# Batch 0 of a spectral-mixing kernel: filter halves copied by GpSimd and DMA, two-bank blocks, and rings in place of pools

## The chip, the cores and the metric

The kernel runs on one core of one Trainium2 chip. The metric is the device time of one execution in microseconds (us). The kernel before takes 776.99 us, the median of three runs (776.98 to 777.12).

The engines are called here as the profile calls them: PE is the TensorE matmul, PEld its weight load, DVE the VectorE, ACT the ScalarE, POOL the GpSimd, SP the SyncE, whose queue only issues transfers. A line number such as L501 is a line of the kernel before; PSUM is the memory that matmuls write, in eight banks of 512 float32 per partition.

## The reference

For eight batches of 3008 tokens with 256 channels, a real Fourier transform along the tokens, a product with a complex filter, and the inverse transform; then, for all 24064 tokens, a layer of width 2048 with a snake activation and a projection back to 256.

```
X = np.fft.rfft(x, axis=1)
F = (filt_r + 1j * filt_i)[None, :, :]
y = np.fft.irfft(X * F, n=x.shape[1], axis=1)
...
h = x @ w_in
s = np.sin(alpha * h)
g = h + s * s / (alpha + 1e-09)
out = g @ w_out
```

## The kernel before, in words

The transform of length 3008 is split as 47 x 64. A first small transform runs over 47 points (`wf_t`), giving 24 classes `s` of real and imaginary parts; a second one runs over 64 points per class (`d_t`), and its result lies with real parts on partitions 0 to 63 and imaginary parts on 64 to 127. There the filter is applied, and the two inverse transforms follow (`e_t`, then `wi_t`). What comes out is `y`, channels on partitions.

**The main loop.** `chunks` are pieces of 512 (or 384) tokens of `y`. For a chunk `k`, `hidden(k, jb)` makes 128 of the 2048 hidden columns: two matmuls into one bank (L601), a cosine on ACT (L605), a combination on DVE (L606). `project(k - 1, u)` multiplies the chunk before with `w2` (L621), ACT copies the result (L630), and POOL's queue stores it. One step of the loop is two `hidden` and the matching `project`. The transforms of batches 1 to 7 are planned into these steps by hand: `put(at, fn)` gives each piece a step number, `slot` issues what is due. Each engine works off its own instructions in the order in which they are issued.

**The head.** Batch 0 has no batch before it to hide beside, so its transform is the head of the program. In order: 16 first matmuls with evictions (L459, L185/L187); four transposes on DVE (`turn`, L473); for 12 blocks of four classes and one half of the channels (`hc`), `forward_0` (four matmuls into one bank of the `hps` pool, L491, then an ACT eviction into `xf0`, L495), `product_0` (one DVE instruction of 1024 elements per partition that multiplies `xf0` with both filter tiles, L501) and `inverse_0` (eight matmuls into a bank of the `fps` pool, L513, then an ACT eviction, L185); two large transposes back (`turn_back`, L473); then the last transform (`last_0`, L403) and the first `hidden`. Blocks 0 to 5 use classes 0 to 11, blocks 6 to 11 classes 12 to 23. `warm_pe(n)` issues n matmuls on zeros that nothing reads (L437). `inverse_table` (L426, L428) makes `e1_0`, the inverse table for the crossed products, by transposing `d_t` and scaling it with -0.125 on ACT.

**The filter.** A real-by-complex product needs the real filter on both partition halves and the imaginary one on both halves, with opposite signs. The load brings each into one half only (`filt_t`, L364: classes 0 to 11 as g = 0, classes 12 to 23 as g = 1). `other_half(g, k)` makes the other half on DVE, by a copy for the real part (L187) and a multiplication with -1 for the imaginary part (L445). The two for g = 0 stand between and behind the four transposes, the two for g = 1 around product 5.

**The weights.** SP's queue loads six parts of `w_in` (L526), the first after the real filter of g = 1 has landed, then four tables and `w_out` (L536). POOL scales `w_in` into `w1` (`weights_in`, L542), held back until the last product of batch 0, and `w_out` into `w2` (`weights_out`, L574).

**Batches 1 to 7** use `forward` (ACT evicts into `xf`, L246, then two transfers on SP's queue swap the partition halves into `xs`, L250), `product` (L257), `cross` (L263, L264) and an inverse. `xf` comes from a pool of three buffers, `xs` of three, `p` of seven. Batch 1 has its twelve `forward` 1.21 steps apart, batch 2 has them 2.2 steps apart, later ones 4.

Of the kernel before, what the change touches and what calls it, by code (L numbers as in the profile page):

```python
# [71 lines left out]
def kernel(  # L72
# [38 lines left out]
    xfpool = pool("xf", 3)  # L111
    ppool = pool("pp", 7)
    xspool = pool("xs", 3)
# [4 lines left out]
    fps = pool("fps", 2, PSUM)  # L118
    hps = pool("hps", 4, PSUM)
    ops = pool("ops", 2, PSUM)  # L120
# [31 lines left out]
    f_t = [filt_t[:, k] for k in range(2)]  # L152

# [35 lines left out]
    class Spectral:  # L189
# [13 lines left out]
        def first(self, i):  # L203
            ch, j = divmod(i, 4)
            ps = fps.tile([128, 512], FP32, name=f"pa_{self.b}_{i}", tag="f")
            marks["pe"] = nc.tensor.matmul(out=ps[0:NK, :], lhsT=wf_t, rhs=self.x[ch][:, 2 * j:2 * j + 2, :],  # L206
                                           start=True, stop=True)
            r0 = 8 * (ch % 2)
            evac(t1_h[ch // 2][0:NK, r0 + 2 * j:r0 + 2 * j + 2, :], ps[0:NK, :])
            if j == 3:  # L210
                nc.sync.dma_start(out=self.d1_rows[:, 8 * ch:8 * ch + 8, :], 
                                  in_=t1_h[ch // 2][0:NK, r0:r0 + 8, :])

        def first_tiled(self, ch):
            r0 = 8 * (ch % 2)
            for q in range(2):
                own, tag = (hps, "h") if q else (fps, "f")
                ps = [own.tile([128, 512], FP32, name=f"pa_{self.b}_{ch}_{q}_{h}", tag=tag) for h in range(2)]
# [19 lines left out]
        def forward(self, u):  # L238
            b = self.b
            ps = fps.tile([128, 2, C], FP32, name=f"pb_{b}_{u}", tag="f")  # L240
# [4 lines left out]
            self.xf[u] = xfpool.tile([128, 2, C], FP16, name=f"xf_{b}_{u}", tag="xf")  # L245
            nc.scalar.copy(out=self.xf[u], in_=ps)  # L246
            if self.fused:
                self.xs[u] = xspool.tile([128, 2, C], FP16, name=f"xs_{b}_{u}", tag="xs")
                for p in range(2):
                    nc.sync.dma_start(out=self.xs[u][64 * p:64 * p + 64, :, :],  # L250
                                      in_=self.xf[u][64 - 64 * p:128 - 64 * p, :, :])

        def product(self, u):
            self.p[u] = []
            for k in range(1 if self.fused else 2):
                pt = ppool.tile([128, 2, C], FP16, name=f"p_{self.b}_{u}_{k}", tag="p")
# [9 lines left out]
        def inverse(self, w):  # L266
# [4 lines left out]
            ps = fps.tile([128, 2, C], FP32, name=f"pc_{b}_{w}", tag="f")  # L271
# [12 lines left out]
        def inverse_tiled(self, w):  # L284
            g = gpool.tile([128, 4, 2, C], FP16, name=f"gt_{self.b}_{w}", tag="g")
            for q in range(2):
                own, tag = (hps, "h") if q else (fps, "f")
                ps = [own.tile([128, 2, C], FP32, name=f"pc_{self.b}_{w}_{q}_{k}", tag=tag) for k in range(2)]
# [20 lines left out]
        def last(self, u):  # L309
# [3 lines left out]
            ps = fps.tile([128, 4, 128], FP32, name=f"pd_{self.b}_{u}", tag="f")  # L313
            psv = ps.rearrange("p a b -> p (a b)")[:, 0:4 * NR].rearrange("p (a r) -> p a r", r=NR)
# [20 lines left out]
    one = cpool.tile([128, 16], BF16)  # L335
    for t in [one] + parts:
        nc.gpsimd.memset(t, 0.0)
# [10 lines left out]
    def spread_alpha(i):  # L348

        ps = hps.tile([128, 4, 128], FP32, name=f"al_bc_{i}", tag="h")  # L350
# [42 lines left out]
    def last_0(n0, n, own=fps, tag="f", spread=False):  # L393

        for cb in range(2):
            made = []

            def one(i, cb=cb, made=made):

                if i == 0:  # L400
                    ps = own.tile([128, 512], FP32, name=f"pd_0_{n0}_{cb}", tag=tag)
                    made.append(ps[:, 0:n * NR].rearrange("p (a r) -> p a r", r=NR))
# [11 lines left out]
    def reciprocals():  # L414

        ps = ops.tile([128, 512], FP32, name="ps_rec", tag="o")
# [3 lines left out]
    def inverse_table(g):  # L420

        gs = slice(8 * g, 8 * g + 8)
        ps = ops.tile([128, 8, 128], FP16, name=f"pse_{g}", tag="o")
# [4 lines left out]
        nc.scalar.mul(e1_0[:, gs, :], ps, -0.125)  # L428

    warmed = []  # L430

    def warm_pe(n):

        warmed.append(n)
        ps = hps.tile([128, 512], FP32, name=f"warm_{len(warmed)}", tag="h")
# [3 lines left out]
    def other_half(g, k, on_act):  # L439

        gs = slice(12 * g, 12 * g + 12)
        if k == 0:
            evac(f_t[0][64:128, gs, :], f_t[0][0:64, gs, :], on_act)
        else:
            nc.vector.tensor_scalar(out=f_t[1][0:64, gs, :], in0=f_t[1][64:128, gs, :],  # L445
                                    scalar1=-1.0, scalar2=None, op0=ALU.mult)
# [9 lines left out]
    for i in range(16):  # L456
        own, tag = (fps, "f") if i % 3 == 2 else (hps, "h")
        ps = own.tile([128, 512], FP32, name=f"pa_0_{i}", tag=tag)
# [21 lines left out]
    for i in range(4):  # L480
        turn(t2_0[i // 2][:, :, 32 * (i % 2):32 * (i % 2) + 32], t1_0[:, :, 32 * i:32 * i + 32])
        if i > 1:
            other_half(0, i - 2, False)
    blocks = [(hc, w) for hc in range(2) for w in range(3)] + [(0, 3), (1, 3), (0, 4), (0, 5), (1, 4), (1, 5)]
    xf0, p0 = {}, {}

    def forward_0(i):
        hc, w = blocks[i]
        ps = hps.tile([128, 4, 128], FP32, name=f"pb_0_{i}", tag="h")
        for j in range(4):  # L490
            nc.tensor.matmul(out=ps[:, j, :], lhsT=d_t[:, 4 * w + j, :],  # L491
                             rhs=t2_0[hc][:, 4 * w + j], start=True, stop=True)
        own, tag = (xspool, "xs") if i % 2 else (xfpool, "xf")
        xf0[i] = own.tile([128, 4, 128], FP16, name=f"xf_0_{i}", tag=tag)
# [3 lines left out]
    def product_0(i):  # L498
        hc, w = blocks[i]
        p0[i] = xpool.tile([128, 2, 4, 128], FP16, name=f"p_0_{i}", tag="x")  # L500
        marks["products"] = nc.vector.tensor_tensor(  # L501
            out=p0[i].rearrange("p f s (k c) -> p f s k c", k=2),
            in0=xf0[i].rearrange("p s (k c) -> p s k c", k=2)[:, None].to_broadcast([128, 2, 4, 2, 64]),
            in1=filt_t[:, :, 4 * w:4 * w + 4].rearrange("p f s (k c) -> p f s k c", k=2)[..., 64 * hc:64 * hc + 64],
            op=ALU.mult)

    def inverse_0(i):
        hc, w = blocks[i]
        ps = fps.tile([128, 4, 128], FP32, name=f"pc_0_{i}", tag="f")
        for j in range(4):  # L510
            s = 4 * w + j
            for k in range(2):
                nc.tensor.matmul(out=ps[:, j, :], rhs=p0[i][:, k, j, :],  # L513
                                 lhsT=e_t[:, s, :] if k == 0 else e1_0[:, s, :],
                                 start=(k == 0), stop=(k == 1))
        evac(g_0[hc][:, 4 * w:4 * w + 4], ps.rearrange("p s (k c) -> p s c k", k=2), not (i in ()))

    after(nc.sync.dma_start(out=wi0_t, in_=wi0_dram.ap()), marks["filt", 0, 1])
    w_in_v = moe_w_in.rearrange("(a p) j -> p a j", p=128)
    w_in32 = []  # L520
    for g in range(6):
# [5 lines left out]
        if g == 0:  # L527
            after(ins, marks["filt", 1, 0])
        marks["w_in"] = ins
# [18 lines left out]
    [inverse_table(g) for g in range(2)]  # L548
    for i in range(6):
        forward_0(i)  # L550
        if i % 3 == 2:
            if i == 2: inverse_table(2)
            warm_pe((4, 0)[i // 3])
    for i in range(13):
        for e in {5: [(1,0,False)],6: [(1,1,False)]}.get(i, ()):
            other_half(*e)
        if i < 12:
            product_0(i)
        if i == 11:
# [3 lines left out]
        if i + 6 < 12:  # L563
            forward_0(i + 6)
        if i == 12:
            turn_back(0)
# [16 lines left out]
    warm_pe(12)  # L583
    last_0(0, 4)
    last_0(4, 2, hps, "h")
# [8 lines left out]
    def hidden(k, jb):  # L594
# [4 lines left out]
        ps = hps.tile([128, 512], FP32, name=f"ph_{k}_{jb}", tag="h")  # L599
# [10 lines left out]
    def project(k, u):  # L610
# [7 lines left out]
        if (t % 2 == 0 or alone) and half == 0:  # L618
            pso[k] = ops.tile([128, 2, C], FP32, name=f"po_{k}_{t}", tag="o")
# [73 lines left out]
    for at, fn in put_later:  # L693
        put(at, fn)

# [3 lines left out]
    for n0, n, at in ((6, 5, 1.5), (11, 4, 11), (15, 4, 13), (19, 4, 15.5), (23, 4, 17), (27, 5, 19)):  # L699
        put(at, last_0, n0, n, fps, "f", True)  # L700
# [91 lines left out]
```

## Time and profile before

| what | value |
|---|---|
| median of three runs | 776.99 us |
| the profiled execution's own time | 779.76 us |
| its span in the trace | 778.0 us |
| PE / DVE / ACT / POOL busy | 98% / 85% / 78% / 48% |
| start of the first `last_0` matmul (L403) | 36.98 us |
| start of the first `hidden` matmul (L601) | 38.53 us |

Busy shares are of the whole span. The head is its first 39 us, where the limits are others than in the rest, so it is read by itself: from the rows in order of time, which give the start, the length, the engine, the line, what is written and read, the count, and in brackets the engine's idle time before and what ended it. The profile is of one execution on the one core.

### The profile page before, as it was taken

How to read it: one execution, taken by the hardware profiler on the slowest of the kernel's cores; microseconds unless marked ns; L12 is line 12 of the kernel's file. 1: busy time of each engine (PE TensorE's matmuls, PEld its weight loads, DVE VectorE, ACT ScalarE, POOL GpSimd, SP SyncE). 2: the span in 40 equal slices, each digit the busy share in tenths (PEclk: the TensorE clock that was granted, in tenths of full speed). 3: DMA queues.
4: the chain of work that ended last, by engine and by line, in shares of the span. 5: the costliest groups of instructions: out<-in, count | busy, mean ns of one | idle time of the engine just before them, and what ended most of it. 6: DMA issues, size and time to landing. Idle time of an engine off the chain costs nothing.

```text
span 778.0 us, 17230 instructions
## 1 busy us (share of the span) xinstructions
PE 764.5 (98%) x6039; PEld 517.0 (66%) x6039; DVE 658.0 (85%) x1174; ACT 610.4 (78%) x1204; POOL 370.4 (48%) x649
## 2 busy tenths in 40 slices
PE   7999999999999999999999999999999999999997
PEld 3757766666666666666666666766666666766665
DVE  6986998999988888898889988898888888787773
ACT  5798888898878877888878787788778787777762
POOL 6355555634555655455464647554454645430000
PEclk9999999999999999999999999999999999999999
DMA  9955578864765428644474536864254322511112
GB/s 223 267 108 160 119 181 242 220 137 124 187 165 133 124 58 219 154 108 127 107 194 121 139 95 145 198 152 120 72 145 110 87 70 56 135 46 34 37 41 56
DMA packets 81518, 101.49 MB, mean 130 GB/s; under 512 B 18884, under 2 KB 60864, under 8 KB 81431
## 3 DMA queue, kind: packets, MB, share of 16 engines
q0 software_dynamic: 27440, 47.29, 26.1%
q1 hardware_dynamic: 53434, 52.79, 25.4%
q8 instruction: 47, 0.77, 0.4%
q10 hardware_dynamic: 557, 0.31, 0.2%
q14 instruction: 40, 0.33, 0.1%
HBM read 56.15 MB, written 46.66 MB: 132 GB/s over the span
## 4 chain that ended last, share of the span: by engine, by line
PE 91%; DVE 5%; ACT 1%; issue 1%; DMA 1%; ACTq 0%; DVEq 0%
PE po L621 40%; PE ph L601 40%; DVE v L606 3%; PE pd L316 2%; PE pb L243 2%; PE pa L222 2%; PE pc L293 1%; ACT cos_all L605 1%; PE pc L513 1%; DMA w<-in_moe_alpha_dram 1%; PE warm L437 1%; PE pb L491 1%; PE pa L459 1%; PE pa L206 0%; PE pd L403 0%
## 5 line engine op out<-in xcount | busy, mean ns | idle before, releaser
L606 DVE SCALAR_TENSOR_TENSOR v<-cos_all,ph 128x512 f16<-128x512 f32 (+1 forms) x768 | 482.5, 671 | 99.2 <-ACT cos_all L605 95.7
L605 ACT ACTIVATE cos_all<-ph 128x512 f32<-128x512 f32 (+1 forms) x768 | 413.9, 600 | 101.8 <-PE ph L601 98.5
L665 POOL DMA_DIRECT2D out_dram<-o x530 | 291.7, 557 | 244.1 <-ACT o L630 215.3
L621 PE MATMUL po<-w,v 128*128 128x256 f16 x3008 | 389.9, 273 | 0.9 <-DVE v L606 0.9
L601 PE MATMUL ph<-y,w 128*128 128x512 f16 (+1 forms) x1536 | 389.1, 375 | 1.3 <-DVE v L606 1.1
L621 PEld LDWEIGHTS <-v 128*128 128x128 f16 x3008 | 289.9, 98 | 85.9 <-DVE v L606 1.5
L601 PEld LDWEIGHTS <-w 128*128 128x128 f16 x1536 | 143.1, 98 | 114.0 <-issue 19.1
L630 ACT COPY o<-po 128x512 f32<-128x512 f32 (+1 forms) x95 | 56.1, 591 | 7.6 <-PE po L621 6.9
L246 ACT CAST xf<-pb 128x512 f16<-128x512 f32 x84 | 51.1, 608 | 2.0 <-PE pb L243 1.2
L185 ACT CAST y<-pd 128x376 f16<-128x376 f32 (+1 forms) x86 | 42.1, 491 | 12.3 <-PE pd L316 8.8
L160 POOL DMA_DIRECT2D x<-in_x_dram x48 | 25.6, 538 | 40.1 <-DVE v L606 26.8
L185 ACT CAST t_h<-pa 128x512 f16<-128x512 f32 (+1 forms) x60 | 32.8, 590 | 12.5 <-PE pa L222 11.3
L316 PEld LDWEIGHTS <-t_a 96*128 96x128 f16 x448 | 31.4, 97 | 12.7
L264 DVE TENSOR_TENSOR p<-p,xs 128x512 f16<-128x512 f16 x84 | 35.7, 425 | 2.9
L263 DVE TENSOR_TENSOR xs<-xs,filt_t 128x512 f16<-128x512 f16 x84 | 35.1, 418 | 1.6 <-DMA xs<-xf 1.6
L257 DVE TENSOR_TENSOR p<-xf,filt_t 128x512 f16<-128x512 f16 x84 | 35.0, 417 | 0.0
L185 ACT CAST gt<-pc 128x512 f16<-128x512 f32 x54 | 28.1, 595 | 8.4 <-PE pc L293 8.4
L187 DVE CAST t_h<-pa 128x512 f16<-128x512 f32 (+1 forms) x52 | 33.5, 682 | 0.2
L243 PE MATMUL pb<-t,d_t 128*128 128x256 f16 x168 | 32.1, 273 | 0.6 <-ACT cos_all L605 0.6
L316 PE MATMUL pd<-wh_t,t_a 96*128 96x94 f16 x384 | 31.8, 204 | 0.0
L235 POOL DMA_DIRECT2D t<-d x28 | 24.4, 874 | 12.0 <-DMA d<-t_h 10.9
L243 PEld LDWEIGHTS <-d_t 128*128 128x128 f16 x168 | 16.3, 98 | 15.1 <-DMA t<-d 0.8
(70 smaller groups left out, 278.0 us busy)
## 6 DMA issues: line engine op xcount, KB each, us to landing
t<-d POOLq DMA_DIRECT2D x28, 384.0 KB, 5.2
xs<-xf SPq DMA_DIRECT2D x168, 64.0 KB
t_a<-d SPq DMA_DIRECT2D x28, 384.0 KB
x<-in_x_dram POOLq DMA_DIRECT2D x50, 188.0 KB, 4.5
d<-t_h SPq DMA_DIRECT2D x48, 192.0 KB
d<-gt SPq DMA_DIRECT2D x36, 256.0 KB
out_dram<-o POOLq DMA_DIRECT2D x91, 64.0 KB, 2.1
out_dram<-o POOLq DMA_DIRECT2D x31, 80.0 KB, 3.6
```

Of the source, the lines that this page charges most:

```text
L185: marks["act"] = nc.scalar.copy(out=dst, in_=src)
L243: nc.tensor.matmul(out=ps[:, i, :], lhsT=d_t[:, s, :], rhs=self.t2[s // 6][:, s % 6, :], start=True, stop=True)
L246: nc.scalar.copy(out=self.xf[u], in_=ps)
L263: nc.vector.tensor_tensor(out=xs, in0=xs, in1=f_t[1][:, 2 * u:2 * u + 2, :], op=ALU.mult)
L264: nc.vector.tensor_tensor(out=p, in0=p, in1=xs, op=ALU.add)
L316: nc.tensor.matmul(out=psv[:, i, :], rhs=wi_t if self.b < TILED else wh_t, start=True, stop=True, lhsT=t4_h[ch // 2][0:NK, n0 % 16 + i, cb ...
L601: nc.tensor.matmul(out=ps[:, 0:n], lhsT=w1[:, cb, jb * 128:jb * 128 + 128], rhs=y_cols[:, cb, c0:c0 + n], start=(cb == 0), stop=(cb == 1))
L605: nc.scalar.activation(out=cs[:, 0:n], in_=ps[:, 0:n], func=AFT.Sin, bias=float(np.pi / 2))
L606: marks["snake"] = nc.vector.scalar_tensor_tensor(out=v[k][:, jb, 0:n], in0=cs[:, 0:n], scalar=-1.0, in1=ps[:, 0:n], op0=ALU.add, op1=ALU. ...
L621: nc.tensor.matmul(out=pso[k][:, t % 2, :], lhsT=v[k][:, jb, 128 * t:128 * t + 128], rhs=w2[:, jb, :], start=(jb == 0), stop=(jb == 15))
L630: copy(out=o[:, i0:t % 2 + 1, :], in_=pso[k][:, i0:t % 2 + 1, :])
L665: queues[i % len(queues)].dma_start(out=bass.AP(tensor=out.tensor, offset=out.offset + t0 * C, ap=[*ap, [1, C]]), in_=o_blk[p0:p0 + rows, :])
```

## The change

- **Filter halves.** `other_half(g, k)` now copies without a sign, as 1536 uint32 elements of 64 partitions. For g = 0 POOL does both copies, issued behind the four transposes. For g = 1 both are transfers on SP's queue: the real one behind the load of `wi0_t` and ahead of `w_in`, the imaginary one between the first and the second part of `w_in`.
- **The sign.** `inverse_table` multiplies with a column `sign` (0.125 on partitions 0 to 63, -0.125 on the others; two memsets on DVE at the start), so that batch 0 needs no negated filter. Batches 1 to 7 do: `negate(g)` does it later, on POOL, in place, at steps 8 and 9 of the main loop.
- **Blocks.** Batch 0 goes in eight blocks of 8 and 4 classes in turn. A block of 8 fills two neighbouring banks; one ACT instruction evicts both. `product_0` is two DVE instructions, one per filter tile. `inverse_0` goes into the two `fps` banks (blocks of 8) or one of the two `ops` banks (blocks of 4). The inverse of block 4 is evicted by DVE, the others by ACT. `forward_0` runs four blocks ahead instead of six.
- **Rings.** One PSUM tile of eight banks, with `Ring.take` handing out banks in turn, replaces the three pools of 2, 4 and 2 banks. One tile `work` of 13 pieces replaces the pools `xf` (3), `xs` (3) and `pp` (7): `xf` now has 2 pieces, `xs` 4, `p` 7; batch 0 uses the same pieces.
- **Warm-up.** `warm_pe(12)` ahead of `last_0` becomes `warm_pe(8)`.

```
+    psum = pool("psum", 1, PSUM).tile([128, 8, 512], FP32, name="psum")
+        def take(self, n=1):
+            at = -(-self.at // n) * n % self.n
+            self.at = (at + n) % self.n
+            return psum[:, self.first + at:self.first + at + n].rearrange("p b c -> p (b c)")
+    fps, hps, ops = Ring(0, 2), Ring(2, 4), Ring(6, 2)
...
+    work = cpool.tile([128, 13, 512], FP16)
+    pieces = work.rearrange("p n (i c) -> p n i c", c=C)
...
-            self.xf[u] = xfpool.tile([128, 2, C], FP16, name=f"xf_{b}_{u}", tag="xf")
+            self.xf[u] = pieces[:, u % 2]
...
-                self.xs[u] = xspool.tile([128, 2, C], FP16, name=f"xs_{b}_{u}", tag="xs")
+                self.xs[u] = pieces[:, 2 + u % 4]
...
-                pt = ppool.tile([128, 2, C], FP16, name=f"p_{self.b}_{u}_{k}", tag="p")
+                pt = pieces[:, 6 + (12 * self.b + u) % 7]
...
-        nc.scalar.mul(e1_0[:, gs, :], ps, -0.125)
+        nc.scalar.mul(e1_0[:, gs, :], ps, sign)
...
-    def other_half(g, k, on_act):
+    def other_half(g, k, copy):
+        src = slice(64 * k, 64 * k + 64)
+        dst = slice(64 - 64 * k, 128 - 64 * k)
         gs = slice(12 * g, 12 * g + 12)
-        if k == 0:
-            evac(f_t[0][64:128, gs, :], f_t[0][0:64, gs, :], on_act)
-        else:
-            nc.vector.tensor_scalar(out=f_t[1][0:64, gs, :], in0=f_t[1][64:128, gs, :],
-                                    scalar1=-1.0, scalar2=None, op0=ALU.mult)
+        return copy(out=filt_t[dst, k, gs].rearrange("p s c -> p (s c)").bitcast(UINT32),
+                    in_=filt_t[src, k, gs].rearrange("p s c -> p (s c)").bitcast(UINT32))
+    def negate(g):
+        gs = slice(12 * g, 12 * g + 12)
+        nc.gpsimd.tensor_scalar(out=f_t[1][0:64, gs, :], in0=f_t[1][0:64, gs, :], scalar1=-1.0, scalar2=None,
+                                op0=ALU.mult)
...
-        if i > 1:
-            other_half(0, i - 2, False)
-    blocks = [(hc, w) for hc in range(2) for w in range(3)] + [(0, 3), (1, 3), (0, 4), (0, 5), (1, 4), (1, 5)]
+    for k in range(2):
+        other_half(0, k, nc.gpsimd.tensor_copy)
+    blocks = [(hc, s0, n) for g in range(2) for hc in range(2) for s0, n in ((12 * g, 8), (12 * g + 8, 4))]
...
+        ps = hps.take(n // 4).rearrange("p (s c) -> p s c", c=128)
+        xf0[i] = work[:, 2 * (i % 6):2 * (i % 6) + n // 4].rearrange("p b (s c) -> p (b s) c", c=128)
...
+        for f in range(2):
+            marks["products"] = nc.vector.tensor_tensor(
+                out=p0[i][:, f].rearrange("p s (k c) -> p s k c", k=2),
+                in0=xf0[i].rearrange("p s (k c) -> p s k c", k=2),
+                in1=f_t[f][:, s0:s0 + n].rearrange("p s (k c) -> p s k c", k=2)[..., 64 * hc:64 * hc + 64],
+                op=ALU.mult)
...
+        ps = (ops if i % 2 else fps).take(n // 4).rearrange("p (s c) -> p s c", c=128)
...
+        evac(g_0[hc][:, s0:s0 + n], ps.rearrange("p s (k c) -> p s c k", k=2), i != 4)
...
     after(nc.sync.dma_start(out=wi0_t, in_=wi0_dram.ap()), marks["filt", 0, 1])
+    other_half(1, 0, nc.sync.dma_start)
...
         if g == 0:
             after(ins, marks["filt", 1, 0])
+            other_half(1, 1, nc.sync.dma_start)
...
+    inverse_table(0)
+    inverse_table(1)
+    forward_0(0)
+    forward_0(1)
+    inverse_table(2)
+    warm_pe(4)
+    forward_0(2)
+    forward_0(3)
+    for i in range(9):
+        if i < 8:
             product_0(i)
-        if i == 11:
+        if i == 7:
             reciprocals()
         if i > 0:
             inverse_0(i - 1)
-        if i + 6 < 12:
-            forward_0(i + 6)
+        if i + 4 < 8:
+            forward_0(i + 4)
+    turn_back(0)
     turn_back(1)
...
-    warm_pe(12)
+    warm_pe(8)
...
+    for g in range(2):
+        put(8 + g, negate, g)
```

## The prediction, made before the result was known

> **What bounds the kernel now.** I read the page's shares and chain first, then the rows of the head in order of time for DVE, ACT and SP, then windows of PE with the granted clock, then ACT's waits around batch 1.
>
> From the page:
>
> ```profile
> PE 764.5 (98%) x6039; PEld 517.0 (66%) x6039; DVE 658.0 (85%) x1174; ACT 610.4 (78%) x1204; POOL 370.4 (48%) x649
> ...
> PE 91%; DVE 5%; ACT 1%; issue 1%; DMA 1%; ACTq 0%; DVEq 0%
> ```
>
> PE is the bound over the span, so the loop pays only for what makes PE idle. What the change does to the head counts by one point: when the last transform of batch 0 (L403, 36.98 us) can start. DVE's rows in order of time:
>
> ```profile
> 18.02 1.20 DVE L473 STREAM_TRANSPOSE t<-t 128x1024 uint32<-128x1024 uint32 x1
> 19.23 0.95 DVE L187 COPY filt_t<-filt_t 64x3072 f16<-64x3072 f16 x1
> 20.20 1.25 DVE L473 STREAM_TRANSPOSE t<-t 128x1024 uint32<-128x1024 uint32 x1
> 21.48 0.96 DVE L445 TENSOR_SCALAR filt_t<-filt_t 64x3072 f16<-64x3072 f16 x1
> 22.54 3.10 DVE L501 TENSOR_TENSOR p<-xf,filt_t 128x1024 f16<-128x1024 f16 x5
> 25.67 0.95 DVE L187 COPY filt_t<-filt_t 64x3072 f16<-64x3072 f16 x1
> ...
> 32.42 4.50 DVE L473 STREAM_TRANSPOSE t_a<-t_h 128x2048 uint32<-128x2048 uint32 x2 [0.16 <-ACT t_h L185]
> ```
>
> DVE is never idle for long from 15.7 to 36.92, and L403 follows 0.06 later: here DVE is the bound. ACT, however, is full beside it:
>
> ```profile
> 17.05 1.94 ACT L428 ACTIVATE t_a<-pse 128x1024 f16<-128x1024 f16 x2 [0.20 <-PE pse L426]
> 22.15 2.05 ACT L495 CAST xf<-pb 128x512 f16<-128x512 f32 x4 [0.78 <-PE pb L491]
> ```
>
> Two starts of 512 elements lie 0.48 apart, (2.05 - 0.61) / 3; two of 1024 lie 0.86 apart (1.94 - 1.08). A block of 1024 saves 0.10 against two of 512.
>
> SP, and two windows of PE (start:end, busy, matmuls, clock, DMA share, GB/s):
>
> ```profile
> 17.86 0.36 SPq L518 DMA_DIRECT2D wi_t<-wi_tbl  x1
> 20.97 3.68 SPq L526 DMA_DIRECT2D w_in<-in_moe_w_in_dram  x6
> ```
> ```profile
> 5.00:9.00 4.00, 2.17 (x9) 0.96 1.07 212
> 9.00:12.00 3.00, 3.00 (x8) 0.50 1.09 311
> ```
>
> 17.86 and 20.97 are when the imaginary filter of g = 0 and the real one of g = 1 had landed. The second window shows that a stretch with PE about half busy was followed by 3 us at half clock.
>
> **The change, part by part.**
>
> *DVE's copies go.* Four instructions, 0.95 + 0.96 + 0.95 + 0.96 = 3.82 us. Added: two 64-row memsets (0.06 each, by the 128x1 memset of L321; they delay the first warm-up matmul, not its successors, which wait for x); products, 12 of 0.62 become 8 of 0.62 and 8 of 0.35 (0.62 less 512 elements at 0.53 us), +0.35; the eviction of block 4, 1.25 (0.69 for 512 elements plus 0.56, by the slope between the y casts of 188 and 376). DVE's own work falls by 2.1 us. The fourth transpose ends at 20.48 instead of 21.45.
>
> *POOL's two copies, 1536 elements each.* No such row. Lower bound 1.4 us: casts of 16 and 128 elements take 0.19 and 0.28, 0.8 ns an element. Upper 3.4: the two-input rows of L542, 2.1 ns an element (768 against 512). I take 1.4, the one-input row. POOL has issued its last load at 16.73: copies end at 18.2 and 19.6, before DVE wants them at 20.5. At 3.4 the second ends at 23.5 and costs about 1 us.
>
> *ACT.* Twenty-four evictions of 512 become 7 of 1024 and 8 of 512: 11.5 to 9.9 us. The pointer `sign` on three tables: 0 to 0.1 each, taken 0.1. From 17.05 ACT must do three tables (2.9), six evictions of 1024 (5.3) and four of 512 (1.9) until the inverse of block 2 has left the two fps banks: 27.2. Block 4's inverse needs these banks, DVE's eviction waits for it, and products 6 and 7 are queued behind that eviction. So without any late transfer: inverse 4 at 27.3 to 28.2, eviction to 29.5, products 6 and 7 (1.94) to 31.45, 0.25 to the transposes as now, 4.5: 36.2, a gain of 0.7.
>
> *SP's copy of the imaginary half, g = 1.* This replaces a DVE instruction that ran at once when its load had landed. The load's last issue on POOL is at 15.5; its semaphore in the trace ends at 24.35, as the page's 8.5 us to landing gives. The copy of 393 KB can be issued no earlier. Lower bound: the fastest swap of batch 1 (64 KB, SP, SBUF to SBUF) took 1.9 us; 329 KB more at the 295 GB/s of 22 to 26 us, 1.1; landed at 27.4. Upper: the first part of `w_in`, 393 KB on the same queue, took 5.1 (20.97 to 26.09 by its semaphore); landed at 29.5. I take 27.9, nearer the lower, since the competing POOL queue has landed its last at 25.1. Then: product 4's second half to 28.5, inverse 4 28.65 to 29.55, eviction to 30.9, products 6 and 7 to 32.85, transposes 33.1 to 37.6. Against 36.92: **0.7 late** (0.2 to 2.3). The real half is issued at 21 and, by the 5.1 above, is there at about 26: in front of that.
>
> *Behind it on SP:* `w_in` 1 to 5 go out 3 us later (issue 24.8 instead of 21.4) behind 786 KB more; the last, landed at 31.8 before, lands near 35. POOL wants part 1 at 34, part 5 at 42 (L542): hidden, with 3 us to spare at part 1. `w_out` (39.2 before) at about 41.5; wanted at 44.1.
>
> *PE's clock.* PE waits from 26.4 to 28.65 and, after inverse 5, from about 29.4 to 32.3. From 29.2 to 32.6 it is busy some 1.1 of 3.4 us, less than the 2.17 of 4 that were followed by half clock. I take it that 3.4 us from 32.6 run at half speed: the rest of inverse 6 to 33.8, inverse 7 to 34.7, the alpha matmuls (24 of 0.056) to 36.7, eight warm-ups of 0.216 to 38.4. L403 is behind these in PE's order: 38.4 instead of 36.98, so the head is **1.4 late**, the clock's 0.8 over DVE's 0.7. Without the fall, PE is through at 36.7 and DVE's 37.6 decides.
>
> The Trainium skill, "TensorE: Matmul & The Clock Gate", Part 1, has a free-running activity window of 3.4 us after which an idle PE runs at 1.2 GHz; the trace agrees (half clock for 3 of 3 us from 9 on). By that rule 1.4 late; with a warm clock 0.7.
>
> *`xf` with two buffers.* Batch 1:
>
> ```profile
> ACT xf L246 <- DMA xs<-xf: 0.4, 1, 0.4
> ```
>
> With three buffers ACT waits once, for 0.4: eviction 9 (98.24) for the swaps of 6 (landed 98.14). With two it waits for the swaps of 7, landed 100.85, 2.4 later; eviction 8 (95.74) for those of 6, 2.4, less 1.2 because the fourth `xs` lets them go out earlier; eviction 10 (101.32) for those of 8, 0.9. Queued behind it on ACT are the cosines, and PE runs on by the banks it still has: at 1.7 takes of two fps banks a step of 2.2 us, about 2.5. So PE loses 0 to 2.4; I take **0.4**, since most lies under PE's lead. Batches 2 to 7 are 2.2 or 4 steps apart: nothing.
>
> *Negation on POOL*, two of 3072 elements at 0.8 ns, 2.6 each (6.5 at 2.1 ns). POOL is idle from 49.7 to 58.8 and the loads of `t` start at 69.6: hidden either way. If the cover were gone, out stores would wait 4 us, which three `o` buffers take.
>
> The Trainium skill, "SBUF — State Buffer", on the shared port pair, has GpSimd and a DVE operation with two SBUF inputs exclude each other; between 49.7 and 60 DVE's operations (L606, one input in PSUM) are none of these, and L606 keeps its 0.6 us beside L542. By that rule nothing is lost here.
>
> Rings leave PE's waits in the loop as they were: in the built program 702 hidden matmuls wait for DVE instead of 705.
>
> **Sum.** Head +1.4, `xf` +0.4: **+1.8 us**. The profiled execution took 779.76 (span 778.0 and 1.76 around it), 2.77 over the median; I put the difference on the median: 778.8.
>
> **Rivals.**
>
> 1. *Nothing measurable.* The transfer lands at 27.4 and the clock holds: head +0.2, `xf` 0 to 0.4, 777.4. For it: inverses 4 to 7 do come in that stretch, and where a window begins is open. Against: the idle 2.9 us before inverse 6.
> 2. *Faster.* DVE becomes the true bound: transfer landed by 26, ACT's starts of 1024 at 0.7. Then DVE's 9.0 us from 20.48 end at 29.5, 0.35 and the transposes follow: 34.35, a gain of 2.6 with nothing lost at `xf`: 774.4. It decides from a landing before 26.9, where ACT's 27.2 takes over (gain 0.7, 776.3). For it: 3.82 us of DVE work on the critical chain really go. Against: the load itself lands at 24.35.
> 3. *Worse.* The transfer takes `w_in`'s 5.1 us, and ACT's waits at `xf` reach PE: +2.3 + 0.8 + 2.4 = 5.5, 782.5.
>
> **How the numbers follow.** 0.2% is 1.55 us, about what a measurement of this kernel can tell from no change. My case (lateness of 1 to 4 us), 0.48, two thirds of it slower by over 0.2%; nothing measurable 0.22; faster 0.20 (0.18 by over 0.2%); worse 0.10. Slower 0.32 + 0.10, rounded up to 0.45 because the second landing bound is the better measured; faster 0.18; same 0.37. The range leaves out the upper half of "worse" and the best of "faster": 775.0 to 781.0; my case alone is 778 to 780.5.
>
> **What would show it.** Right: no DVE instruction on `filt_t` alone; DVE idle by some 2 us before product 4's second half, released by a DMA on `filt_t`; PE at 0.5 in a window after 32; L403 at 38; ACT waiting for `xs<-xf` over 2 us in batch 1. Wrong: products without a gap, or the gap put down to PE or ACT; the clock at 1.0 throughout; L403 before 36.98. The step I trust least is the landing of that one transfer, then the clock.

## The result, and the profile after

The changed kernel takes 789.09 us (median of five, 787.54 to 790.42) against 776.99 (776.96 to 778.01): **ratio 1.0141, 95% interval 1.0128 to 1.0155**. The forecast had the sign and missed the size: 778.8, with 781.0 as the end of its range.

From here on a line number is a line of the kernel whose rows are shown. DVE's rows of the kernel after, in order of time (start, length, then the row; in brackets the idle time before it and what ended it):

```profile
13.74 2.37 DVE L482 STREAM_TRANSPOSE t_a<-t 128x1024 uint32<-128x1024 uint32 x2 [0.17 <-ACT t L194]
16.04 2.33 DVE L482 STREAM_TRANSPOSE t<-t 128x1024 uint32<-128x1024 uint32 x2
19.16 0.69 DVE L509 TENSOR_TENSOR p<-work,filt_t 128x1024 f16<-128x1024 f16 x1 [0.79 <-POOL filt_t L449]
21.21 3.24 DVE L509 TENSOR_TENSOR p<-work,filt_t 128x1024 f16<-128x1024 f16 x7 [1.35 <-POOL filt_t L449]
27.92 0.69 DVE L509 TENSOR_TENSOR p<-work,filt_t 128x1024 f16<-128x1024 f16 x1 [3.47 <-DMA filt_t<-filt_t]
31.46 1.36 DVE L509 TENSOR_TENSOR p<-work,filt_t 128x1024 f16<-128x1024 f16 x3 [2.86 <-DMA filt_t<-filt_t]
34.07 1.23 DVE L196 CAST t_h<-psum 128x1024 f16<-128x1024 f32 x1 [1.25 <-PE psum L520]
...
39.94 2.31 DVE L482 STREAM_TRANSPOSE t_a<-t_h 128x2048 uint32<-128x2048 uint32 x1 [0.47 <-ACT t_h L194]
```

The four instructions on `filt_t` alone are gone, as the change says. In their place DVE waits 0.79 and 1.35 us for POOL's copies and 3.47 and 2.86 us for SP's: 8.47 us. The last transform (L411) starts at 42.94, the first `hidden` at 44.41.

SP's issues of the kernel after:

```profile
21.91 0.55 SPq L449 DMA_DIRECT2D filt_t<-filt_t  x1
22.50 0.58 SPq L534 DMA_DIRECT2D w_in<-in_moe_w_in_dram  x1
24.01 0.47 SPq L449 DMA_DIRECT2D filt_t<-filt_t  x1
24.52 3.94 SPq L534 DMA_DIRECT2D w_in<-in_moe_w_in_dram  x5
```

By their semaphores the two copies landed at 27.80 and 31.34, that is 5.9 and 7.3 us after their issue, and DVE goes on 0.12 later each time. Windows of the kernel after (start:end and length, then the busy time of PE, PEld, DVE, ACT and POOL, the granted clock, DMA share, GB/s):

```profile
24.00:28.00 4.00, 2.89 (x41) 2.72 (x38) 0.53 (x3) 4.00 (x7) 0.00 (x0) 1.00 1.00 238
28.00:32.00 4.00, 0.22 (x1) 0.13 (x2) 1.14 (x2) 0.24 (x1) 0.00 (x0) 0.83 1.04 303
32.00:36.00 4.00, 2.87 (x25) 2.67 (x25) 2.75 (x6) 0.59 (x1) 0.00 (x0) 0.50 0.88 268
36.00:40.00 4.00, 3.66 (x34) 3.50 (x34) 3.53 (x6) 1.56 (x2) 2.59 (x2) 0.50 0.94 287
```

PE starves from 28 to 32, and from 30.63 to 40.87 it has half clock. It works off its warm-ups late, and L411 starts at 42.94, 0.69 after DVE's last transpose (42.25).

**Against which execution.** The profiled execution of the kernel before was 2.77 us over the median, so the kernel before was profiled once more, unchanged.

> The kernel before once more, unchanged, for its profile. Theory A (its profiled execution of 779.76 was 2.77 over the median since the clock fell to half at 8.70 to 12.11 us): without that window the transposes start at 13.4 to 13.7, the last transform at 34.5 to 35, the loop's curve is flat against the first profile, 777. Theory B (the 2.77 lay elsewhere): the head as in the first profile.

It took 776.47 us. DVE's rows in it:

```profile
13.34 2.37 DVE L473 STREAM_TRANSPOSE t_a<-t 128x1024 uint32<-128x1024 uint32 x2 [0.16 <-ACT t L185]
...
20.25 3.10 DVE L501 TENSOR_TENSOR p<-xf,filt_t 128x1024 f16<-128x1024 f16 x5
...
25.09 0.96 DVE L445 TENSOR_SCALAR filt_t<-filt_t 64x3072 f16<-64x3072 f16 x1
...
30.14 4.50 DVE L473 STREAM_TRANSPOSE t_a<-t_h 128x2048 uint32<-128x2048 uint32 x2 [0.17 <-ACT t_h L185]
```

The transposes start at 13.34 and not 15.7, and the last transform at 34.70 and not 36.98: theory A for 2.31 us of it. (The expectation of a loop without any difference held but for 0.78 us at the 76th `hidden` matmul.) The clock of PE, half from 8.70 to 12.11 in the first profile, was full here throughout. This second profile is the base for what follows. In it the n-th `hidden` matmul of both kernels can be compared: the changed kernel starts the first one **8.19 us** later, and by the 272nd it is 12.45 later, which stays to the end (12.47). So 8.2 us are lost in the head and **4.3 us** between 46 and 180 us, and nothing after that.

### The profile page after: what moved, and what is told of

The parts are those of the page before. It is cut to its first block, busy times and chain, and to the rows that moved or that the text cites. A ratio compares the mean times of both kernels' runs of the same rounds, so it can differ in the third digit from the quotient of the medians.

```text
span 787.3 us, 17280 instructions
## 1 busy us (share of the span) xinstructions
PE 766.4 (97%) x6035; PEld 519.6 (66%) x6035; DVE 656.5 (83%) x1177; ACT 609.4 (77%) x1195; POOL 389.5 (49%) x653
## 4 chain that ended last, share of the span: by engine, by line
PE 86%; DVE 5%; DMA 4%; ACT 2%; issue 1%; POOL 0%; ACTq 0%; SPq 0%; DVEq 0%; POOLq 0%
PE psum L629 39%; PE psum L609 38%; DVE v L614 4%; PE psum L322 2%; PE psum L251 2%; PE psum L230 2%; DMA d_t<-d_tbl 1%; ACT cos_all L613 1%; PE psum L300 1%; DMA filt_t<-in_filt_i_dram 1%; DMA filt_t<-filt_t 1%; DMA out_dram<-o 1%; PE psum L520 1%; PE psum L215 0%; DVE t_h L196 0%
## 5 line engine op out<-in xcount | busy, mean ns | idle before, releaser
L614 DVE SCALAR_TENSOR_TENSOR v<-cos_all,psum 128x512 f16<-128x512 f32 (+1 forms) x768 | 483.1, 672 | 99.3 <-ACT cos_all L613 95.6
L613 ACT ACTIVATE cos_all<-psum 128x512 f32<-128x512 f32 (+1 forms) x768 | 413.8, 599 | 102.1 <-PE psum L609 99.1
L609 PE MATMUL psum<-y,w 128*128 128x512 f16 (+1 forms) x1536 | 389.3, 375 | 1.6 <-DVE v L614 1.5
L629 PE MATMUL psum<-w,v 128*128 128x256 f16 x3008 | 389.8, 273 | 0.7 <-DVE v L614 0.6
L638 ACT COPY o<-psum 128x512 f32<-128x512 f32 (+1 forms) x95 | 56.2, 591 | 7.6 <-PE psum L629 6.0
L194 ACT CAST t_h<-psum 128x512 f16<-128x512 f32 (+2 forms) x67 | 38.4, 615 | 22.1 <-PE psum L230 10.7
L254 ACT CAST work<-psum 128x512 f16<-128x512 f32 x84 | 50.9, 606 | 4.5 <-DVE work L272 2.0
L194 ACT CAST y<-psum 128x376 f16<-128x376 f32 (+1 forms) x86 | 41.8, 487 | 11.2 <-PE psum L322 8.8
L272 DVE TENSOR_TENSOR work<-work 128x512 f16<-128x512 f16 x84 | 35.7, 425 | 2.9
L271 DVE TENSOR_TENSOR work<-work,filt_t 128x512 f16<-128x512 f16 x84 | 35.3, 420 | 2.7 <-DMA work<-work 2.7
L265 DVE TENSOR_TENSOR work<-work,filt_t 128x512 f16<-128x512 f16 x84 | 35.1, 419 | 0.7 <-ACT work L254 0.7
```

The source lines that it names most:

```text
L194: marks["act"] = nc.scalar.copy(out=dst, in_=src)
L271: nc.vector.tensor_tensor(out=xs, in0=xs, in1=f_t[1][:, 2 * u:2 * u + 2, :], op=ALU.mult)
L272: nc.vector.tensor_tensor(out=p, in0=p, in1=xs, op=ALU.add)
L609: nc.tensor.matmul(out=ps[:, 0:n], lhsT=w1[:, cb, jb * 128:jb * 128 + 128], rhs=y_cols[:, cb, c0:c0 + n], start=(cb == 0), stop=(cb == 1))
L613: nc.scalar.activation(out=cs[:, 0:n], in_=ps[:, 0:n], func=AFT.Sin, bias=float(np.pi / 2))
L614: marks["snake"] = nc.vector.scalar_tensor_tensor(out=v[k][:, jb, 0:n], in0=cs[:, 0:n], scalar=-1.0, in1=ps[:, 0:n], op0=ALU.add, op1=ALU. ...
```

## The experiments

The lateness columns are the first `hidden` matmul, and what the loop adds to it, each against the second profile of the kernel before. They are of one profiled execution each, the medians of all. The turn of `evac` in the last row is explained with the last experiment.

| kernel | median us | ratio to before, 95% | head late | loop adds |
|---|---|---|---|---|
| changed | 789.09 | 1.0128 to 1.0155 | 8.19 | 4.28 |
| g = 1 copied by POOL | 782.93 | 1.0043 to 1.0090 | 2.51 | 4.27 |
| g = 1 copied by DVE | 783.64 | 1.0054 to 1.0103 | 2.07 | 6.02 |
| SP's copies ahead of `w_in` | 785.71 | 1.0092 to 1.0122 | 5.42 | 4.85 |
| no negation | 790.41 | 1.0160 to 1.0186 | 7.60 | 7.37 |
| `xf` with three pieces | 788.20 | 1.0130 to 1.0156 | 9.32 | 3.71 |
| g = 1 by DVE and `xf` with three | 779.87 | 1.0024 to 1.0042 | 0.98 | 2.42 |
| before, PSUM rings only | 779.20 | 1.0011 to 1.0039 | 0.05 | 2.24 |
| before, real halves by POOL | 779.42 | 1.0025 to 1.0053 | -0.66 | 3.42 |
| the same, turn of `evac` kept | 777.07 | 0.9987 to 1.0009 | -0.27 | 0.06 |

### SP's transfers taken out

```
-    other_half(1, 0, nc.sync.dma_start)
...
-            other_half(1, 1, nc.sync.dma_start)
+    for g in range(2):
+        for k in range(2):
+            other_half(g, k, nc.gpsimd.tensor_copy)      # or, for g = 1, nc.vector.tensor_copy ahead of product 4
```

> The changed kernel, with the two filter halves of classes 12 to 23 copied by POOL right behind those of classes 0 to 11, and no transfer on SP's queue. Theory 1 (the two SP transfers, landed at 27.8 and 31.3 us, are the head's loss of 6 us): POOL's copy takes 1.75 us as its two in the changed kernel did (3.51), so the halves are there at about 23.7 and 25.8; product 4 runs on without a gap, the last transform of batch 0 starts at 37 to 38 us instead of 43.1, and the time falls by 5 to 6 us to 783 to 784. Rival (the transfer only hides ACT's and PE's lateness behind it, the clock above all): the start stays at 41 or later and the time at 787 or more. A second question: products with two SBUF inputs beside POOL copies. If the two exclude each other, some products start up to 1.75 us late; if not, their 0.62 us spacing holds.

> The changed kernel, with the same two halves copied by DVE (0.95 us each, no sign) in front of product 4. Theory 1: the imaginary half is there at 25 us, DVE carries 1.9 us more than in the changed kernel without a wait; the last transform starts at about 38 and the time is 783 to 785. Rival as for the POOL copies: 787 or more. If the POOL copies were slower than this one, POOL and DVE stand in each other's way.

Measured: 782.93 and 783.64, so 6.2 and 5.5 us of the 12.1 are gone. The head keeps 2.5 and 2.1 of its 8.2. SP's two transfers are the largest cause, 5.7 to 6.1 us. With DVE's copies, DVE's rows are:

```profile
18.63 0.69 DVE L509 TENSOR_TENSOR p<-work,filt_t 128x1024 f16<-128x1024 f16 x1 [0.61 <-POOL filt_t L449]
20.68 3.24 DVE L509 TENSOR_TENSOR p<-work,filt_t 128x1024 f16<-128x1024 f16 x7 [1.35 <-POOL filt_t L449]
23.95 1.94 DVE L449 COPY filt_t<-filt_t 64x1536 uint32<-64x1536 uint32 x2
25.92 1.96 DVE L509 TENSOR_TENSOR p<-work,filt_t 128x1024 f16<-128x1024 f16 x4
```

DVE still waits 1.96 us for POOL's copies of g = 0, as much as the two DVE copies that they replace. With all four on POOL, these two rows (DVE, then POOL) show another price:

```profile
18.44 8.87 DVE L510 TENSOR_TENSOR p<-work,filt_t 128x1024 f16<-128x1024 f16 x10 [0.43 <-POOL filt_t L449]
```
```profile
20.93 1.75 POOL L449 COPY filt_t<-filt_t 64x1536 uint32<-64x1536 uint32 x1 [1.06 <-DMA filt_t<-in_filt_r_dram]
23.17 1.72 POOL L449 COPY filt_t<-filt_t 64x1536 uint32<-64x1536 uint32 x1 [0.48 <-DMA filt_t<-in_filt_i_dram]
```

Each of the products that lay beside a POOL copy took 1.68 to 1.98 us, where such a product alone takes 0.69: the one at 21.28 ended at 22.96, 0.28 behind the copy's 22.68. The Trainium skill, "SBUF — State Buffer", section "SBUF: two separate sides", says that GpSimd and a DVE operation with two SBUF inputs hold the shared port pair in turn and never together; these rows agree.

### Why the transfers land late

```
     other_half(1, 0, nc.sync.dma_start)
+    other_half(1, 1, nc.sync.dma_start)        # and no longer behind the first part of w_in
```

> The changed kernel with both SP copies of the filter ahead of the first part of w_in. Theory A (the copies are late because w_in, on the same queue, shares the engines with them): the imaginary copy, issued at 24, lands in 4 us or less, 28.0; last transform at 39 to 40, 785.5 to 786.5. Theory B (the price is that of their own packets, 456 to 487 ns each where a transfer over all 128 partitions has 237 to 260, and of the wait behind the real copy): packets stay at 450 ns and over, landing at 29.5 or later, last transform at 41 or later, 787 to 789.

SP's issues and DVE's rows of this kernel:

```profile
22.71 2.36 SPq L449 DMA_DIRECT2D filt_t<-filt_t  x2
25.12 4.33 SPq L535 DMA_DIRECT2D w_in<-in_moe_w_in_dram  x6
```
```profile
27.89 0.69 DVE L509 TENSOR_TENSOR p<-work,filt_t 128x1024 f16<-128x1024 f16 x1 [4.41 <-DMA filt_t<-filt_t]
29.35 1.36 DVE L509 TENSOR_TENSOR p<-work,filt_t 128x1024 f16<-128x1024 f16 x3 [0.77 <-DMA filt_t<-filt_t]
```

785.71 us, and DVE has the imaginary half at 29.35 and not at 31.46. Neither theory holds alone. Sharing the queue with `w_in` is worth 2.8 us of the head (8.19 to 5.42); the other 3.3 (5.42 to the 2.07 without transfers) stay with the transfers themselves. The records of packets say why. The two copies are 128 packets of 6144 bytes, which took 452 ns on average here (435 in the changed kernel: 466 for the real copy, 405 for the imaginary one). Packets of the same 6144 bytes of loads over 128 partitions took 239 to 256 ns on average from 10 to 12 us. An estimate from these: spread evenly over 16 engines, the copies are eight packets of 0.45 us each, 3.6 us before anything else. The Trainium skill, "SBUF — State Buffer", section "Door 1: The DMA port swizzle", has the speed of a transfer depend on how many of the memory's 16 ports its partitions reach, and by its table partitions 0 to 63 reach eight and 64 to 127 the other eight. The factor of about 1.8 between the two averages agrees. Those loads of the filter whose packets are as long, over 32 partitions, had 449 to 472 ns a packet on average in the trace of before already (14 to 16 and 18 to 20 us): the price was there to be read.

### The loop: negation, `xf`, rings

```
-    for g in range(2):
-        put(8 + g, negate, g)
```

> The changed kernel without the two negations on POOL (8 us each at 54.8 to 70.7 us); it leaves out the sign of half of the imaginary filter for batches 1 to 7, so what it computes for these is not the reference. In the changed kernel the loop loses some 3.5 us against the kernel before, about 1.45 of it by the PSUM rings. Theory A (the negation keeps POOL's queue from issuing stores for 12 us, the output buffers run out, ACT and then PE wait): 1 to 2 us of this goes, 787 to 788, and the gap to the curve of the rings alone at 128 to 176 matmuls shrinks by over half. Theory B (nothing waits for POOL there, as the prediction had it): 789.1, within 0.5.

790.41 us, not faster, and 0.8 over what theory B allows. POOL's rows of the changed kernel show how large the negation is:

```profile
54.77 15.91 POOL L455 TENSOR_SCALAR filt_t<-filt_t 64x3072 f16<-64x3072 f16 x2
70.64 3.73 POOL L673 DMA_DIRECT2D out_dram<-o  x7
```

Eight us each, and the first out stores start at 70.64 us and not at 56.45, some 5 us more than the loop is late by then. Yet nobody waits: without it the curve of the loop is the same, within 0.1, up to the 144th matmul. So far theory B. (Past it this run loses 1.8 us and, at 155 us, 1.5 us more, where PE waits 0.81 for a load of x; the run says only that taking the negation away gains nothing.)

```
-            self.xf[u] = pieces[:, u % 2]
+            self.xf[u] = pieces[:, u % 3]
-                self.xs[u] = pieces[:, 2 + u % 4]
+                self.xs[u] = pieces[:, 3 + u % 4]
-                pt = pieces[:, 6 + (12 * self.b + u) % 7]
+                pt = pieces[:, 7 + u % 6]
```

A first try kept `xs` at three pieces:

> The changed kernel with three xf and three xs pieces instead of two and four, as before the change. From the end of the head to 182 us the changed kernel loses another 3.5 us against the one before, then nothing more. Theory 2a (two xf pieces make ACT wait in batch 1): ACT's waits at the eviction into work fall from 3.4 us to under 1 and 1 to 3 us come back, 786 to 788. Theories 2b (bank order of the rings) and 2c (negation on POOL): no more than 0.5 us comes back, 788.5 to 790.

806.41 us. In it the forward of step u + 3 is issued ahead of the cross of step u, which still needs the same piece of `xs`; part of what it computes is therefore not the reference's, and it tells nothing of ACT's waits. The diff shown is the second try:

> The changed kernel with the 13 pieces dealt otherwise: xf 3 (as before the change), xs 4, p 6; six p are enough by the order of issue. Theory A (ACT waits for the swaps at xf with two pieces, as the prediction priced at 0.4, bounds 0 to 2.4): 786.7 to 788.5, and the shift of the hidden matmuls stops growing in batch 1's stretch (95 to 110 us). Theory B (ACT's waits lie under PE's lead): 789.1, within 0.5, and the same curve.

788.20 us. ACT's waits from 44 to 125 us (in total, times, longest) in the changed kernel, then in this one:

```profile
ACT work L254 <- DVE work L272: 2.0, 1, 2.0
...
ACT work L254 <- PE psum L251: 0.6, 1, 0.6
```
```profile
ACT work L254 <- PE psum L251: 0.6, 1, 0.6
```

The wait of 2.0 us of an eviction into `xf` is gone, and with it the curve's steps: the changed kernel loses 0.26 and 0.46 around the 130th matmul (109 to 112 us), and 1.15 from the 264th to the 272nd (175 to 181 us); this one neither. The two steps have different holders.

The first is the wait of 2.0. The profile names DVE's cross (L272), but the cross doesn't touch `xf`, and in the kernel with g = 1 copied by DVE the same wait has another name:

```profile
ACT work L254 <- DMA work<-work: 1.9, 1, 1.9
```

In both kernels the transfer's semaphore is complete 0.10 before the eviction starts (106.53 and 106.63, 100.31 and 100.41). So the swap held it, as theory A says. The second step lies in batch 2 of the changed kernel:

```profile
175.85 0.75 DVE L265 TENSOR_TENSOR work<-work,filt_t 128x512 f16<-128x512 f16 x2
```
```profile
176.35 0.59 ACT L254 CAST work<-psum 128x512 f16<-128x512 f32 x1 [1.24 <-PE psum L322]
```

The matmul named there had ended 0.6 earlier. The first of the two products reads the piece that this eviction overwrites, and ends at 176.27, 0.08 before it starts; in the four other kernels here with two pieces of `xf` it starts 0.07 to 0.08 behind that product as well, after the same wait of 1.24. With three pieces the eviction doesn't wait, and comes before that product. So here DVE's product held it.

Theory A, though the time alone (0.9 less) wouldn't show it: its profiled execution had a head 1.1 later and 1.4 us lost at one x load. The clean comparison is with both late causes out:

> The changed kernel without the two late causes: both halves of g = 1 copied by DVE and xf with three pieces (xs 4, p 6). If the causes add up (SP's copies some 6 us of the head, xf 2.0 of the loop, rings 1.5, blocks and POOL's g = 0 copies the rest): 783.64 less 2.0, 781.2 to 782.0, and the curve of the loop is that of the rings alone. If the loop's loss at xf came from the late head, it is as without xf's third piece: 783.2 to 784.

779.87 us, 3.8 under the same kernel with two pieces and 1.3 under the expectation. The loop adds 2.42, what the rings alone add. The two profiled executions lie 4.7 apart: 1.74 are the steps named above; 1.09 lie in the head, of which DVE's last transpose has 0.35 and PE the rest (its clock stayed full from 32 to 36 here, and was 0.57 there); 1.87 come between the 400th and the 800th matmul of the kernel with two pieces, almost all at one stall around 319 us, where DVE's cross waits 3.40 us for a swap to land and PE 1.57 for DVE. Why that swap landed late is not known. By the curves `xf` costs 1.7 to 1.9 us.

The rings by themselves, in the kernel before:

```
+    fps, hps, ops = Ring(0, 2), Ring(2, 4), Ring(6, 2)
...
-            ps = fps.tile([128, 512], FP32, name=f"pa_{self.b}_{i}", tag="f")
+            ps = fps.take()
```

> The kernel before, with the PSUM rings in place of its three pools and nothing else. Theory 2b (a strict rotation of the banks makes PE wait for the slower of two evictions where the pool gave another bank; at 56.9 us PE waited 1.40 for DVE in the changed kernel, at the same place 0.42 for ACT before): 1 to 3.5 us slower than before, 778 to 780.5. Theories 2a and 2c: within 0.3 us of before, 776.7 to 777.3.

779.20: 2.3 us slower, in four steps, at the 36th matmul, between the 48th and the 64th, at the 82nd and at the 184th, which every kernel with rings and this turn of `evac` has (the turn is explained below). PE at the first step, in the kernel before (second profile) and with rings:

```profile
47.75 0.38 PE L206 MATMUL pa<-x,wf_t 94*96 94x512 f16 x1 [0.43 <-ACT t_h L185]
```
```profile
48.78 0.38 PE L216 MATMUL psum<-x,wf_t 94*96 94x512 f16 x1 [1.40 <-DVE t_h L197]
```

At the same place the pool gives the bank that ACT emptied at 47.70; the ring gives the one whose turn it is, which DVE empties behind its `v` work from 48.05 to 48.73. One microsecond goes at this take.

### One part of the change alone, and a hidden turn

```
-            evac(f_t[0][64:128, gs, :], f_t[0][0:64, gs, :], on_act)
+            nc.gpsimd.tensor_copy(...)      # the same halves as 1536 uint32
```

> The kernel before with one part of the change alone: the two real halves are copied by POOL (1.75 us each) and no longer by DVE (0.95 each); sign, imaginary halves, blocks, pools and SP's queue stay. Theory A (DVE is the bound of the head): the copy of g = 0 at 17 to 19 us lies beside a transpose and costs nothing, so 0.95 goes in full; the one of g = 1 runs at 21 to 23 beside the first product, which is slowed by up to 1.3 (1.98 for 0.69 in the run with both copies on POOL) and gives back most of the second 0.95: last transform 0.6 to 1.5 earlier, 775.5 to 776.4. Theory B (ACT is as full as DVE and is next): gain under 0.3, 776.7 to 777.0, DVE idle before products, released by ACT or PE.

779.42, slower by 2.4, which neither theory had. The head was 0.66 early, but the loop lost 3.4. `evac` counts its calls, and where the caller names no engine, every third goes to DVE. Two calls fewer in the head turn all such evictions of the loop by one place. (The changed kernel has six calls fewer, two copies and four evictions of inverses, which is two full turns: its loop has the deal of the kernel before.) So the counter was stepped on by hand:

> The kernel before with the two real halves copied by POOL, as in the run before, but with the counter in evac stepped on as if the two copies still went through it. Without them the counter reached the loop two steps short, so that every eviction of the loop that is dealt out by turns went to another engine than in the kernel before. Theory A (that shift, not the copies on POOL, cost the 2.6 us that the loop lost): the shift of the hidden matmuls stays flat in the loop and only the head's 0.7 remains: 775.9 to 776.7. Theory B (POOL's copies or the head's earlier end cost the loop): the curve rises by 2 to 3 us as in the run before, 779 to 779.6.

777.07 beside 777.43 of the kernel before: no difference that can be measured, and the loop's curve is flat. The turn alone is 2.4 us by the two medians, 2.7 with each against its own runs of the kernel before. Of 1.9 us of DVE work removed, 0.27 arrive. DVE's rows, then POOL's:

```profile
19.38 3.10 DVE L503 TENSOR_TENSOR p<-xf,filt_t 128x1024 f16<-128x1024 f16 x5 [0.19 <-issue]
24.04 0.69 DVE L503 TENSOR_TENSOR p<-xf,filt_t 128x1024 f16<-128x1024 f16 x1 [1.56 <-ACT t_h L185]
```
```profile
22.54 1.46 POOL L444 COPY filt_t<-filt_t 64x1536 uint32<-64x1536 uint32 x1 [4.28 <-DVE p L503]
```

The first product starts 0.87 earlier than in the second profile of before (19.38 and not 20.25), so the copy of g = 0 on POOL is worth nearly its 0.95. Then product 5 waits 1.56. The profile names ACT, but that eviction ended at 24.05, when the product had started; POOL's copy of g = 1, which the product needs, fills the wait and ends at 24.00. The copy itself was released by the fifth product (ended 22.48), behind which it stands in the program. So it didn't run beside the products, as theory A had it, but in the chain in place of DVE's copy: between the fifth product and the next lie 1.56 us, where it was 1.02. That ACT is the next bound, theory B, is not shown.

Whether another turn suits the rings better was tried on the kernel with g = 1 by DVE and three pieces of `xf`:

```
-    flip = [0]
+    flip = [1]        # and [2]
```

> The changed kernel with g = 1 copied by DVE and xf with three pieces, and the counter in evac started one step later, so that the loop's evictions are dealt to ACT and DVE in another turn. The rings still cost 2.4 us of its loop, seen first where a first matmul of batch 1 waits 1.40 for the bank that DVE has yet to empty, while the kernel before took the bank that ACT had emptied. Theory A (the ring forces one bank, and the cost is which engine was dealt that bank's eviction): another turn moves the time by over 1 us, and one of the two other turns is faster than 779.87, down to 777.5. Theory B (the fixed order of the banks costs the same under any deal): 779.5 to 780.5 in both.

> The same with the counter two steps later. Theory A: one of the two turns is 1 us or more under 779.87; theory B: 779.5 to 780.5.

> The kernel before with the counter started two steps later and nothing else. One step later (by the run with POOL's copies and without their two calls of evac) cost 2.35 us. Theory A (the turn in use is the one that fits): 778.5 to 780. Theory B (only that one turn was bad): 776.9 to 777.6.

782.68 and 780.25 with rings, 778.69 in the kernel before (ratio 1.0010 to 1.0029). The deal of the evictions moves the time by up to 2.8 us. The turn in use is the best of three without rings, and with them no other is better (780.25 can't be told apart from 779.87). Theory A is right that the deal matters and wrong that another would make this kernel faster. But the price of the rings belongs to the deal: two steps later, the loop adds 2.76 with rings and 2.78 without, nothing between them, where the turn in use has 2.42 and 0. By the medians 780.25 and 778.69 differ by 1.6, by the two profiles by 0.6, all in the head. No version measured here is faster than the kernel before.

## Why the prediction missed

The sum of +1.8 us against 12.1:

- **SP's copy of the imaginary half: the term that failed.** It was taken to land at 27.9, with 29.5 as the upper bound; it landed at 31.34, 7.3 us after an issue (24.01) that was foreseen. The bounds came from a 64-KB swap and from `w_in`, which spreads over 128 partitions; the rows nearest in shape, the filter's loads of 32 partitions, were not used. The real half, "there at about 26: in front of that", landed at 27.80 and stopped DVE for 3.47 us. With its followers this makes 5.7 to 6.1 us of the head, where the sum had 1.4. Step by step, the head is 8.2 late and not 1.4 (starts of the last transform): 3.4 more by the landing, 2.3 by the profile that was taken as the base (below), 1.2 because 10.9 us and not 9.7 lie between the landing and DVE's last transpose, where PE has half clock and DVE waits 1.25 for PE and 0.47 for ACT, and 0.1 less behind that.
- **PE's clock: right.** Half clock came after the gap, and L411 0.69 behind DVE's last transpose (0.8 was said). The gap was longer, and the half clock lasted 10.24 us, three stretches of 3.41, where the sum had one. The rule of the Trainium skill, "TensorE: Matmul & The Clock Gate", Part 1, cited there agrees with these rows, as far as they go.
- **POOL's two copies: said to be hidden, cost 2.1 us of waiting.** They took 1.46 and 1.99 us (1.4 taken, bounds 1.4 to 3.4), the second beside a product of two SBUF inputs, and the last ended at 21.18 (19.6 said). More weighs that DVE wanted them at 18.4, not at 20.5: the profile read was of an execution with a head 2.3 us late, while the loads that the copies wait for come by their own time. The wait is put down to POOL, and stands in the runs without SP's transfers too.
- **The difference of 2.77 us put on the median.** This step belongs to the same error. An execution that is late at the start hides what comes late from elsewhere; in a usual one that cover is gone, so the forecast change was 2.3 us too small from the start.
- **DVE's gain of 2.1 and ACT's of 0.7.** Not seen in any run. With POOL's real halves alone, 1.9 us less on DVE gave 0.27: 0.87 of it arrived at the first product, and 0.54 went again where a product waited for POOL's second copy. Whether ACT follows right behind DVE, as the prediction's list for ACT has it, no run here shows.
- **`xf` with two pieces: half of it foreseen.** 0.4 taken, 1.7 to 1.9 measured, inside its bounds of 0 to 2.4. In batch 1 one eviction waits 2.0 us for a swap as foreseen (2.4 said; the waits of 1.2 and 0.9 at its neighbours did not come), and PE loses 0.6 to 0.7. The larger half, 1.15, came at 175 to 181 us in batch 2, for which the prediction had said "nothing": it had asked only when the swaps have read a piece, and there DVE's product, planned late, held it. That the total lies inside the bounds is luck.
- **The rings: said to cost nothing, cost 2.3 at the turn in use.** Counting which engine PE waits for (702 against 705) didn't show it; what changed is which bank is taken next and when that bank is emptied.
- **The negation: hidden, as said,** though it is 8 us each where 2.6 was taken and 6.5 was the upper bound.

By the profiles: transfers 5.7 to 6.1 (the clock's fall behind them included), other head causes 2.1 to 2.5, rings 2.4, `xf` 1.9, together the 12.5 us. Of the head's 2.1 with DVE's copies, 1.1 were not there in the execution whose clock stayed up, 0.35 of that before PE's last stretch; the last 1.0 lies with POOL's g = 0 copies and the blocks, which were not taken apart further. Rivals 1 and 2 asked for a landing by 27.4 and 26.9 (by the prediction's own steps 26.5 for the second, a slip of the sum that decides nothing), and no run with these transfers had one before 29.2. Rival 3 ("worse", 0.10) had the right mechanism and still stopped at 5.1 us of landing.

## What to carry to other kernels

Before a sum is made against a profiled execution, see where that execution differs from the median: lateness at its start is slack that a usual execution doesn't have. Price a transfer by rows of the same number of partitions as well as bytes, and ask what shares its queue. Before a buffer is taken away, list every reader of it, engines as well as transfers. When the profile names an engine that ends a wait, compare its end with the start of what waited. When calls are removed or a pool becomes a ring, look for what the code deals out in turns: counters and bank orders reach far past the edited place, and here they moved the time by 2.3 to 2.8 us.

## What the runs showed of the hardware

- SBUF to SBUF transfers over 64 partitions: packets of 6144 bytes at 435 to 452 ns on average, as against 239 to 256 for loads over 128 partitions; 393 KB took 5.9 and 7.3 us from issue to landing beside `w_in`.
- A POOL copy of 64 x 1536 uint32 takes 1.46 us beside DVE's transposes and 1.72 to 2.01 beside products; a DVE product of two SBUF inputs beside it takes 1.68 to 1.98 us for 0.69.
- POOL's multiplication of 64 x 3072 f16 by a constant takes 7.95 us, 2.6 ns an element per partition, where DVE took 0.96.
- PE at half clock came in whole windows of 3.41 us: 8.70 to 12.11 in the first profile of before, 30.63 to 40.87 after (three of them). The two profiles of the kernel before, with the first window and without it, differ by 2.31 us at the first `hidden` matmul.
